# Long retention score products in all four quarters of the TensorE array

## Chip, cores, metric

One core of a Trainium2 chip. The metric is device time in microseconds (us) of one execution, median of several. The profiler's span of an execution is about 2 us shorter than its time.

## The reference

The first half is a retention layer over 4 batches, 8 heads, 768 tokens and head size 64; the second is a feed-forward layer with a leaky ReLU on 3072 tokens.

```python
for t in range(S):                       # gamma: one decay per head
    state = gamma * state + einsum('bhd,bhe->bhde', k[:, :, t], v[:, :, t])
    y[:, :, t] = scale * einsum('bhd,bhde->bhe', q[:, :, t], state)
x = y.transpose(0, 2, 1, 3).reshape(B * S, H * D)
h = x @ w_in                             # 512 -> 2048
out = maximum(0.01 * h, h) @ w_out       # 2048 -> 512
```

## The kernel before

The tokens go in 6 chunks of 128. Per chunk and batch the retention is: **scores** (keys by queries in the chunk, masked so that no query sees a later key), **reads** (state by queries), **values** (masked scores by v, added onto the reads in PSUM) and **state** (k by v). A key half of 64 tokens meets queries of 128 or, for the later half, 64 tokens, so a head has one long (128 columns) and one short (64 columns) score product. Two heads (j = 0, 1) lie in the two halves of the partitions.

```python
def scores_to(x, ps):
    for a in range(HP):                                   # HP = 4 pairs of heads
        for j in range(2):                                # long: rows j, columns j
            nc.tensor.matmul(halves(ps[j])[ts(j, 64), :, a, :],
                             lhsT=x[ts(j, 64), 1, a, 0:64], rhs=x[ts(j, 64), 0, a, :])
        for j in range(2):                                # short: rows j, columns 1 - j
            nc.tensor.matmul(halves(ps[j])[ts(1 - j, 64), 1, a, :],
                             lhsT=x[ts(j, 64), 1, a, 64:], rhs=x[ts(j, 64), 0, a, 64:])

def visit(c, b):                                          # a "plain visit", cut
    for f in (reads, first_values, last_values, state):
        for i in range(2):
            f(c, b + i)
    ...

def products_in_turn(b):                                  # the same four for chunk 1
    for f in (reads, first_values, last_values, state):
        for i in range(2):
            f(1, b + i)
```

Most batches of chunks 2 to 5 go through another form (a "visit with scores"): scores of a coming batch, reads of two batches, scores of another, then values and state. It is laid between the feed-forward products, which fill TensorE for the rest. In the profiles their groups are named A to D, with `_h` for the first feed-forward product and `_o` for the second. B_h, where it reads t, differences that DVE (VectorE) makes from the attention's output x, has to wait for DVE.

## Time and profile before

| | before |
|---|---|
| time, us | 664.34 |
| span of the profiled execution, us | 662.3 |
| TensorE busy | 99% |
| DVE busy | 57% |
| ScalarE busy | 27% |

A group line has the line of code, engine, operation, tiles and count, then busy time, mean ns of one, idle time ahead of it and what ended that. A line of the chain has start, length and what ran; the chain is followed back from the last instruction, so its pieces add up to the span. The prediction shows most lines of the profile before. Three more will be compared below, all from the chain in order of time: the products of the second pair of batches in chunk 1, and a later group B_h.

```profile
43.19 1.03 PE yp L224 x32
44.23 0.46 PE yp L241 x32
44.69 1.08 PE yp L249 x32
45.77 0.93 PE yp L264 x32
...
351.12 1.99 PE B_h L570 x8
```

L224 are the reads, L241 the first values, L249 the last values, L264 the state: 3.52 us from the first read to the next group, for two batches and without a pause. An undisturbed B_h group takes 1.73.

### The profile page before, as it was taken

To read this page: it belongs to the slowest core of one execution; us is meant where nothing else is said; L and a number is where in the kernel's file an instruction comes from. 1 tells how busy PE (TensorE), PEld (TensorE's weight loads), DVE (VectorE), ACT (ScalarE), POOL (GpSimd) and SP (SyncE) were. 2 spreads that over 40 slices of the span, in tenths; PEclk is the share of its full clock that TensorE was granted. 3 is DMA by queue.
4 is the path that set the end of the run, shared out by engine and by line. 5 is a ranking of instruction groups with operands and counts; after the bars stand their busy time and mean duration, and the time that the engine had idled before them with its cause. 6 is when DMAs were issued, how large, how long until landed. Compare 5 with 4: busy or idle time off the path is not lost.

```text
span 662.3 us, 11362 instructions
## 1 busy us (share of the span) xinstructions
PE 655.2 (99%) x4921; PEld 571.7 (86%) x4921; DVE 377.1 (57%) x635; ACT 176.3 (27%) x323; POOL 21.0 (3%) x25
## 2 busy tenths in 40 slices
PE   8999999999999999999999999999999999999998
PEld 5788888888888888888888888888888888888886
DVE  5789969889889594344437414537434344431342
ACT  4854555255261002202102211300220210221210
POOL 1000000000000020001001001000000100000000
PEclk9999999999999999999999999999999999999999
DMA  9921312322422650030023003005000101000001
GB/s 337 394 100 33 126 65 65 123 68 80 143 65 70 246 194 1 1 96 34 1 72 120 1 1 129 0 13 180 0 1 22 44 1 49 17 0 1 1 0 64
DMA packets 15761, 48.99 MB, mean 74 GB/s; under 512 B 1752, under 2 KB 2008, under 8 KB 15712
## 3 DMA queue, kind: packets, MB, share of 16 engines
q1 hardware_dynamic: 15408, 47.45, 20.6%
q8 instruction: 39, 0.64, 0.4%
q10 hardware_dynamic: 304, 0.81, 0.3%
q14 instruction: 10, 0.08, 0.0%
HBM read 41.97 MB, written 6.29 MB: 73 GB/s over the span
## 4 chain that ended last, share of the span: by engine, by line
PE 96%; ACT 1%; DVE 1%; DMA 1%; issue 0%; DVEq 0%
PE B_o L570 13%; PE A_o L570 13%; PE C_o L570 13%; PE A_h L570 12%; PE B_h L570 12%; PE C_h L570 12%; PE D_o L570 6%; PE D_h L570 6%; PE ap L176 2%; PE yp L249 2%; PE d L592 1%; PE yp L224 1%; PE sp L264 1%; DMA t<-decay_dram 1%; PE yp L241 1%; PE yp L264 0%
## 5 line engine op out<-in xcount | busy, mean ns | idle before, releaser
L570 PE MATMUL A_h<-x,w 128*128 128x256 f32 x368 | 87.7, 381 | 0.0
L570 PEld LDWEIGHTS A_h<-x,w 128*128 128x128 f32 x368 | 69.3, 190 | 9.7 <-issue 0.2
L570 PE MATMUL A_o<-g,w 128*128 128x256 f32 x288 | 68.1, 379 | 0.0
L516 DVE TENSOR_TENSOR m<-m,B_h 128x512 f32<-128x512 f32 x23 | 15.8, 686 | 88.4 <-PE B_h L570 88.4
L570 PEld LDWEIGHTS A_o<-g,w 128*128 128x128 f32 x288 | 54.6, 190 | 7.5
L610 ACT COPY m<-A_h 128x512 f32<-128x512 f32 x23 | 13.5, 586 | 174.5 <-PE A_h L570 154.3
L605 ACT ACTIVATE g<-g 128x512 f32<-128x512 f32 x69 | 42.0, 630 | 66.0 <-DVE g L516 66.0
L516 DVE TENSOR_TENSOR m<-m,B_o 128x512 f32<-128x512 f32 x16 | 11.0, 685 | 64.0 <-PE B_o L570 63.9
L570 PE MATMUL B_h<-t,w 128*128 128x256 f32 x184 | 44.3, 381 | 0.0
L570 PE MATMUL D_h<-t,w 128*128 128x256 f32 x184 | 43.5, 379 | 0.0
L570 PE MATMUL C_h<-x,w 128*128 128x256 f32 x184 | 43.5, 379 | 0.0
L570 PE MATMUL C_h<-t,w 128*128 128x256 f32 x184 | 43.5, 379 | 0.0
L570 PE MATMUL B_h<-x,w 128*128 128x256 f32 x184 | 43.5, 379 | 0.0
L570 PEld LDWEIGHTS B_h<-t,w 128*128 128x128 f32 x184 | 34.6, 190 | 6.0 <-DVE t L519 1.2
L570 PEld LDWEIGHTS D_h<-t,w 128*128 128x128 f32 x184 | 35.0, 190 | 4.8
L570 PEld LDWEIGHTS C_h<-x,w 128*128 128x128 f32 x184 | 35.0, 190 | 4.8
L570 PEld LDWEIGHTS C_h<-t,w 128*128 128x128 f32 x184 | 35.0, 190 | 4.8
L570 PEld LDWEIGHTS B_h<-x,w 128*128 128x128 f32 x184 | 35.0, 190 | 4.8
L150 POOL TENSOR_TENSOR kv<-kv,dec 128x512 f32<-128x512 f32 x18 | 19.9, 1105 | 496.4 <-DMA kv<-in_kv_dram 246.7
L519 DVE TENSOR_TENSOR gd<-g,gd 128x512 f32<-128x512 f32 x48 | 33.2, 692 | 1.7
L570 PE MATMUL B_o<-g,w 128*128 128x256 f32 x144 | 34.0, 379 | 0.0
L570 PE MATMUL C_o<-gd,w 128*128 128x256 f32 x144 | 34.0, 379 | 0.0
(137 smaller groups left out, 1060.8 us busy)
## 6 DMA issues: line engine op xcount, KB each, us to landing
raw<-in_weights_dram SPq DMA_DIRECT2D x31, 512.0 KB, 3.8
kv<-in_kv_dram SPq DMA_DIRECT2D x17, 512.0 KB, 5.0
out_dram<-o SPq DMA_DIRECT2D x23, 256.0 KB, 2.1
qk<-in_qk_dram SPq DMA_DIRECT2D x10, 512.0 KB, 4.6
o<-in_qk_dram SPq DMA_DIRECT2D x8, 512.0 KB, 4.6
in<-in_qk_dram SPq DMA_DIRECT2D x5, 512.0 KB, 8.5
in<-in_kv_dram SPq DMA_DIRECT2D x3, 512.0 KB, 8.1
in<-in_kv_dram SPq DMA_DIRECT2D x4, 256.0 KB, 8.1
```

The costliest lines, as they stand in the source:

```text
L150: engine.tensor_tensor(out=v, in0=v, in1=gk.unsqueeze(2).to_broadcast([128, H, D]), op=ALU.mult)
L176: nc.tensor.matmul(halves(ps[j])[ts(j, 64), :, a, :], lhsT=x[ts(j, 64), 1, a, 0:64], rhs=x[ts(j, 64), 0, a, :])
L224: nc.tensor.matmul(ps[ts(i, 64), j, m, :], lhsT=st[b][ts(j, 64), a, :], rhs=x[ts(j, 64), 0, a, :], start=(m == 0), stop=False, skip_group_ ...
L241: nc.tensor.matmul(ps[ts(i, 64), j, m, 0:64], lhsT=y[ts(j, 64), 1, 2 * a + j, :], rhs=am[ts(j, 64), 0, a, :], start=(c == 0 and m == 0), s ...
L249: nc.tensor.matmul(ps[ts(i, 64), j, m, 64:], lhsT=y[:, 1, 2 * a + j, :], rhs=am[:, 1 + j, a, :], start=False, stop=True, skip_group_check= ...
L264: nc.tensor.matmul(sp[ts(j, 64), a, :], lhsT=y[:, 0, 2 * a + j, :], rhs=y[:, 1, 2 * a + j, :], start=start, stop=True, skip_group_check=True)
L516: nc.vector.tensor_tensor(out=out, in0=a, in1=b, op=ALU.add)
L519: nc.vector.tensor_tensor(out=out, in0=a, in1=b, op=ALU.subtract)
L570: nc.tensor.matmul(half, lhsT=block(w, sa)[:, k, ts(i, 128)], rhs=rhs[:, k, :], start=(first and (i == 0 or split) and n == 0 and k == 0), ...
L592: nc.tensor.matmul(banks[r][:, i, :], lhsT=block(2 * u, r + 2 * kh)[:, k, ts(i, 128)], rhs=x[:, 2 * kh + th, k, :], start=(step == 0 and i ...
L605: nc.scalar.activation(g[:, i], g[:, i], AF.Prelu, alpha=0.01)
L610: nc.scalar.copy(out=got["m1"], in_=ps)
```

## The change

The intent: the long products of heads alternate between the diagonal quarters of the array (rows and columns of the same half) and the crossing ones (`s = i ^ j`, 0 or 1 by the head), so that each quarter of the array gets two long and two short products per batch instead of four of one kind. Two heads of opposite `s` then fit in three columns of 64 instead of four, so that one mask instruction covers what took three. The price: the first values now read from the other row half than the reads, into the same PSUM bank. So they go after the last values, a small ScalarE copy is put behind the reads to make TensorE finish them, and chunk 1 does one batch at a time.

```diff
     def scores_to(x, ps):
-        for a in range(HP):
-            ... (as above)
+        for m in range(HP // 2):
+            for i in range(2):
+                for late in range(2):
+                    for j in range(2):
+                        s, a = i ^ j, 2 * m + i
+                        to = (ps[j][ts(1 - s, 64), m, 1 + s] if late else
+                              ps[j][ts(s, 64), m, 0 : 2 + s : 1 + s])
+                        nc.tensor.matmul(to, lhsT=x[ts(j, 64), 1, a, ts(late, 64)],
+                                         rhs=x[ts(j, 64), 0, a, late * 64 :])
     def masked(c, b):                    # and masked_apart likewise
-        nc.vector.tensor_tensor(out=am[:, 1:3], ...)      # 128x512
-        for j in range(2):
-            masked_first(am, ps[:, j], j)                 # 64x256
+        nc.vector.tensor_tensor(out=am..., in0=scores[c, b]..., in1=mask..., op=ALU.mult)  # 128x768
     def reads(c, b):
         ...
+        nc.scalar.copy(out=between, in_=ps[:, :, 0 : HP // 2, 0:1])
     def first_values(c, b):
-                    lhsT=y[ts(j, 64), 1, 2 * a + j, :], rhs=am[ts(j, 64), 0, a, :]
+                    lhsT=y[ts(s, 64), 1, 2 * a + j, :], rhs=am[ts(s, 64), j, m, 0]
     def visit(c, b):
-        for f in (reads, first_values, last_values, state):
+        for f in (reads, last_values, first_values, state):
     def products_in_turn(b):
-        for f in (reads, first_values, last_values, state):
-            for i in range(2):
-                f(1, b + i)
+        reads(1, b)
+        values(1, b)                      # last values, then first values
+        reads(1, b + 1)
+        values(1, b + 1)
+        state(1, b)
+        state(1, b + 1)
```

## The prediction

> **What bounds the kernel now.** I read the page first (busy shares and the chain that ended last), then the groups by form, then the timeline around the score products, then the chain in order of time around each stage of the attention part.
>
> ```profile
> PE 655.2 (99%) x4921; PEld 571.7 (86%) x4921; DVE 377.1 (57%) x635; ACT 176.3 (27%) x323; POOL 21.0 (3%) x25
> PE 96%; ACT 1%; DVE 1%; DMA 1%; issue 0%; DVEq 0%
> ```
>
> TensorE (PE) is 99% busy and makes up 96% of the chain that set the end. So TensorE's own time counts one for one, and a saving elsewhere counts only where TensorE waits. TensorE waits in few places: the start (about 7 us), one wait of 1.8 us for a mask at 34 us, and three small ones at the weight load of B_h.
>
> The score products are these groups (176 of 384 instructions each; the rest read other tiles in the same shape):
>
> ```profile
> L176 PE MATMUL ap<-qk 64*64 64x128 f32 x176 | 11.6, 272 | 0.6 <-DMA qk<-in_qk_dram 0.6
> L179 PE MATMUL ap<-qk 64*64 64x64 f32 x176 | 9.6, 237 | 0.0
> ```
>
> The busy times of 11.6 and 9.6 us must not be added up as cost: the two kinds run at the same time. The timeline shows how they overlap:
>
> ```profile
> 230.97 0.28 PE L176 MATMUL ap<-o 64*64 64x128 f32 x2
> 230.98 0.27 PE L179 MATMUL ap<-o 64*64 64x64 f32 x2
> 231.08 0.28 PE L176 MATMUL ap<-o 64*64 64x128 f32 x2
> 231.09 0.23 PE L179 MATMUL ap<-o 64*64 64x64 f32 x2
> 231.19 0.28 PE L176 MATMUL ap<-o 64*64 64x128 f32 x2
> ```
>
> Two long products (128 columns) start together every 0.109 us, and the short ones (64 columns) start beside them. Before, the long ones all lie in two of the array's four 64x64 quarters, the short ones in the other two. A batch has 4 long products per quarter, each recorded as two instructions, so a long quarter is occupied 8 x 0.109 = 0.87 us per batch; the short quarters are idle about half of that. The chain agrees: both batches at 230.55 to 232.45 took 1.90 us, which is 16 x 0.109 = 1.74 plus 0.16 at the entry.
>
> The chain of one plain visit (two batches) prices the other products:
>
> ```profile
> 213.03 1.03 PE yp L224 x32
> 214.06 0.46 PE yp L241 x32
> 214.53 1.08 PE yp L249 x32
> 215.61 0.93 PE yp L264 x32
> ```
>
> The reads (L224, 128 columns) take 0.87 us where they follow other products of the same tile shape (at 237 us), and 1.03 here after full-array products: 0.16 for the change of shape. The first-half values (L241) follow in the same shape: 0.46, that is 14.4 ns per instruction, or 57.5 ns per short instruction in each quarter. L249 (128x64) after 64x64 is 1.08, L264 after L249 only 0.93: again 0.15 for the change. A full-array group of 8 costs 1.92 instead of 1.73 after small ones, 0.19. I use 0.16 per change.
>
> **What the Trainium skill says.** "TensorEngine Tiling (Array Packing)", Key Properties: tiles operate independently, and a change of tiling mode drains TensorE. The trace agrees: four quarters at once (the reads: 32 instructions in 0.87 us, 27 ns each, a quarter of 0.109), and 0.15 to 0.19 us per change of shape. "PSUM — Partial Sum Buffer", PSUM bank collisions: two writes from different row tiles into one bank and quadrant at once are an error. That explains the added ScalarE copy: the first-half values now come from the other row half than the reads into the same bank, so something must make TensorE finish the reads first. No run here shows the error itself. The same page, Engine vs sequencer instructions: ScalarE's queue is strict FIFO, so the copy stands behind whatever ScalarE has queued; in the trace ScalarE's long runs of work from 9.7 to 24.9 and 26.9 to 38.4 us are in program order.
>
> **The change, part by part.**
>
> Scores. The new order gives each quarter 2 long and 2 short products per batch: 4 x 0.109 + 4 x 0.056 = 0.66 us instead of 0.87, if a quarter can go on without the others. The order of issue is two long, two short on the crossing quarters, two long there, two short; with as little as one instruction queued per quarter behind the running one this packs without holes. Saving 0.21 us per batch. There are 24 batches: 16 of chunks 2 to 5 sit where TensorE is continuously busy, 4 of chunk 1 too; of chunk 0 only one counts (the others stand before waits for the decay table or for ScalarE's chain, which ends in w at 19.2 us). 21 x 0.21 = 4.5 us gross.
>
> Masks. Three DVE instructions per batch become one:
>
> ```profile
> L201 DVE TENSOR_TENSOR am<-ap,mask x12: 681/691/692, 7.0 to 233.1; 128x512 f32<-128x512 f32 x12
> L342 DVE TENSOR_TENSOR am<-ap,mask x24: 403/422/427, 237.2 to 511.6; 128x256 f32<-128x256 f32 x24
> L212 DVE TENSOR_TENSOR am<-ap,mask x48: 403/416/428, 7.6 to 512.0; 64x256 f32<-64x256 f32 x48
> ```
>
> 512 columns take 0.69 and 1024 take 1.22 us (the states at 25.1), so 768 take an estimated 0.96, against some 1.46 for the three back to back. DVE is not the bound, so this counts only at DVE waits: B_h waits for t in the three visits that also make differences (B_h 1.99 instead of 1.73, 0.26 each), and there one late mask stands ahead of t: 0.67 becomes about 0.48 (384 columns). Saving 3 x 0.19 = 0.6.
>
> The order of values in plain visits. Reads, last, first, state changes shape twice more than reads, first, last, state: 2 x 0.16 in each of the two plain visits of chunks 2 and 5. Cost 0.6. The visits with scores keep their order, and the next score product (0.66) stands between reads and values, so the copy is hidden there.
>
> The copy. In the trace a ScalarE copy of nearly this size is
>
> ```profile
> 7.63 0.17 ACT L807 COPY dec<-tables 128x12 f32<-128x12 f32 x1 [3.88 <-PE tables L804]
> ```
>
> 0.17 us, starting 0.04 after the products. From the last read's start: 0.27 to its end, 0.04, 0.17, some 0.05 back, and a weight load of 0.13 before the next product: about 0.6 after the reads stop issuing, in place of the 0.16 of a change of shape. In plain visits the second batch's reads cover it nearly (0.1 per visit, 0.2 in all). In chunk 1, now one batch at a time, nothing stands between: about 0.45 exposed per batch.
>
> Chunk 1. Per pair of batches without any stall: before 1.03 + 0.46 + 1.08 + 0.93 = 3.50. After: reads 0.60, last 0.62, first 0.39, the same three again at 0.44, 0.62, 0.39, state 1.08: 4.1, plus 2 x 0.45 exposed copy: 5.0. So the second pair loses 1.5. The first pair had this wait:
>
> ```profile
> 34.30 0.67 PE L224 MATMUL yp<-in,states 64*64 64x128 f32 x16 [1.77 <-DVE am L212]
> ```
>
> It goes, because the second mask ends some 1.5 us earlier and the first batch's values no longer stand behind it. But ScalarE is busy with weight conversion until about 32.3, and the first copy queues behind it: some 0.35 more. First pair: 5.5 before (31.95 to 37.45), about 5.35 after; gain 0.15.
>
> Chunk 0. Score and spread 0.21 earlier, which moves ScalarE's chain from 9.7 us on; one change of shape less before 24.5: 0.16. This 0.37 contains the one batch counted above.
>
> Sum. Start to 50 us: -0.37 (chunk 0), -0.85 (four scores of chunk 1), -0.15 and +1.5 (products): +0.1. After: -0.85 (four scores in output steps), -2.5 (twelve in visits with scores), -0.6 (B_h waits), +0.8 (plain visits): -3.1. Total -3.0: 664.35 becomes **661.3 us**, 0.5% less.
>
> **Rivals.**
>
> 1. The quarters are not independent: TensorE issues in order, and mixed long and short products wait for each other as pairs. For it: the skill's page on TensorE ("TensorE: Matmul & The Clock Gate", Part 3) calls matmuls strict FIFO in start and end. Against it: the trace has reads starting in idle quarters (236.74) before two earlier long score products (236.84), and short products hidden fully beside long ones. With no gain in the scores the total would be +1.4: 665.8. With half, 663.5.
>
> 2. The copy costs more than I give it in chunk 1, because ScalarE's queue then waits for TensorE (about 1.5 us idle between the two copies) and pushes decays and weight conversion back into TensorE's path. For it: ScalarE is busy 6.32 of the 6.45 us from 31.0 to 37.45. Against it: ScalarE is idle 4.8 us before 43.2. Some 1 to 2 us worse: 662.3 to 663.3.
>
> 3. DVE's saving of 0.5 us per batch is worth more in the first 50 us than I count: the converted weights and masks come earlier, and the chunk 1 stalls are smaller because some of the copy hides under shape changes that drain anyway. Then 660.
>
> **Range and chances.** The score term is firm to 0.5 if quarters are independent (I give that 85%). The chunk 1 term is the loose one, plus or minus 1. So 8 in 10: **659.7 to 663.0**. All of the attention products cost some 10% of the span, so a change of 2% (13 us) either way is almost out of reach: faster by over 2% 0.01, within 2% 0.98, slower 0.01.
>
> **What would show it.** Right: in the visits the long and short score products interleave so that 32 instructions take about 0.66 us in the chain (two batches at an output step about 1.5 instead of 1.90); B_h near 1.8; plain visits about 3.9 instead of 3.5; the 1.77 us mask wait gone; and in chunk 1 four waits of TensorE for ScalarE at last values, of 0.4 to 1 us. Wrong: score stages still 0.87 per batch (rival 1); TensorE waiting for decays or weights after 36 us (rival 2); the stages from 30 to 47 us shorter than before by more than 2 us (rival 3), or new waits in the visits with scores.

## The result, and the profile after

The changed kernel took 661.01 us (median of 6 runs, 660.91 to 661.24), the kernel before 664.34 in the same rounds: ratio 0.9952, 95% interval 0.9939 to 0.9965. The forecast was 661.3.

The page of the changed kernel, busy shares:

```profile
PE 652.0 (99%) x4921; PEld 568.4 (86%) x4921; DVE 360.5 (55%) x587; ACT 179.4 (27%) x343; POOL 20.4 (3%) x25
```

TensorE has as many instructions as before and 3.2 us less busy time, and it still is 96% of the chain: its work got denser. The chain in order of time shows where. First a score stage of two batches, then the plain visit of chunk 2 (L219 are the reads now), then the later B_h group:

```profile
230.48 1.49 PE ap L182 x48
...
212.65 1.03 PE yp L219 x32
213.69 1.08 PE yp L249 x32
214.77 0.62 PE yp L241 x32
215.39 1.08 PE yp L264 x32
...
349.29 1.81 PE B_h L571 x8
```

Scores went from 1.90 to 1.49 us, B_h from 1.99 to 1.81, and the plain visit from 3.50 up to 3.82: L241 and L264 each pay 0.15 to 0.16 more, because the tile shape changes ahead of each. The second pair of chunk 1:

```profile
41.78 0.64 PE yp L219 x16
42.42 0.02 issue
42.44 0.17 ACT between L224
42.62 0.04 issue
42.66 0.69 PE yp L249 x16
43.34 0.39 PE yp L241 x16
43.74 0.49 PE yp L219 x15
...
44.51 0.69 PE yp L249 x16
45.20 0.39 PE yp L241 x16
45.59 1.08 PE yp L264 x32
```

Here the ScalarE copy stands in the chain between the reads and the last values, and the pair takes 4.89 us instead of 3.52. (ACT is ScalarE.) One line of the timeline shows the longest such wait, where the copy queued behind ScalarE's weight conversion:

```profile
32.42 0.69 PE L249 MATMUL yp<-am,in 128*64 128x64 f32 x16 [0.70 <-ACT between L224]
```

The sum by place, from the chains of the two profiled executions: up to 48.6 us the gain is 0.03 us (48.63 against 48.60); there the scores' and the mask's gain in chunks 0 and 1 (1.0 us up to 37.4, 0.4 more by 39.8) is given back by the second pair. After that: four scores in two output steps -0.8, six visits with scores -0.39 each (the one at 236 from 5.24 to 4.85, the whole of it in its two scores), three B_h groups -0.19 each, and the two plain visits +0.31 in chunk 2 and +0.16 in chunk 5 (549.29 to 551.87 us before, 545.90 to 548.64 after). Chunk 5 has no state products, so there the new order adds one change of tile shape and not two. Together these make -3.3, against the measured -3.2.

### The profile page after: what moved, and what is told of

It is laid out like the page before. It is cut to its first block, busy times and chain, and to the rows that moved or that the text cites. A ratio compares the mean times of both kernels' runs of the same rounds, so it can differ in the third digit from the quotient of the medians.

```text
span 659.0 us, 11325 instructions
## 1 busy us (share of the span) xinstructions
PE 652.0 (99%) x4921; PEld 568.4 (86%) x4921; DVE 360.5 (55%) x587; ACT 179.4 (27%) x343; POOL 20.4 (3%) x25
## 4 chain that ended last, share of the span: by engine, by line
PE 96%; ACT 2%; DMA 1%; issue 0%; DVE 0%; ACTq 0%
PE B_o L571 13%; PE A_o L571 13%; PE C_o L571 13%; PE A_h L571 12%; PE B_h L571 12%; PE C_h L571 12%; PE D_o L571 6%; PE D_h L571 6%; PE ap L182 2%; PE yp L249 2%; PE yp L219 1%; PE d L593 1%; PE yp L241 1%; PE sp L264 1%; DMA qk<-in_qk_dram 1%; ACT in L154 1%
## 5 line engine op out<-in xcount | busy, mean ns | idle before, releaser
L571 PE MATMUL B_o<-gd,w 128*128 128x256 f32 x144 | 34.1, 379 | 0.0
```

Of the source, the lines that this page charges most:

```text
L571: nc.tensor.matmul(half, lhsT=block(w, sa)[:, k, ts(i, 128)], rhs=rhs[:, k, :], start=(first and (i == 0 or split) and n == 0 and k == 0), ...
```

## The experiments

Each kernel ran in 5 rounds beside the kernel before on its chip. The changed kernel itself ran again in the first set as a control:

> The changed kernel itself, unedited, so that the other runs of this chip have it beside them. Every theory expects 0.995 of the kernel before (661.0 us).

Measured 660.95 us, ratio 0.9952. As expected.

**Is it the even share, or the order of issue?**

```diff
-        for m in range(HP // 2):
-            for i in range(2):
-                for late in range(2):
-                    for j in range(2):
+        for cross in range(2):
+            for m in range(HP // 2):
+                for i in range(2):
+                    for j in range(2):
+                        late = i ^ cross
```

> The same score products, to the same places, in another order: all products of the two diagonal quarters of a batch first, then all of the two crossing quarters. Work per quarter is unchanged (2 long, 2 short). Theory A: the even share of work is enough, as each quarter takes its products from a deep queue: score stages stay at 0.65 us per batch, time 661.0. Theory B: TensorE issues in order and only one to three instructions queue behind a quarter's running one, so the gain comes from the alternation in the order of issue as much as from the even share: by that model 0.84 to 1.1 us per batch, so some 21 x 0.2 to 0.45 = 4 to 9 us slower than the changed kernel, 665 to 670.

Measured 666.76 us (ratio 1.0044), 5.8 us slower than the control and slower than the kernel before. Theory B holds. The chain, at the same score stage:

```profile
231.99 2.01 PE ap L183 x53
```

2.01 us instead of 1.49, with the same work in every quarter. A finer grouping was tried as well:

```diff
         for m in range(HP // 2):
-            for i in range(2):
-                for late in range(2):
+            for cross in range(2):
+                for i in range(2):
                     for j in range(2):
+                        late = i ^ cross
```

> As the run named order, but the diagonal quarters go first only within four heads at a time: blocks of eight instructions per side instead of sixteen. By the model of a queue of about three instructions per quarter (which fits the run named order, 2.01 us for two batches) such blocks cost 0 to 0.06 us per batch: 0 to 1.2 us slower than the changed kernel. Rival: any grouping costs in proportion, half of what order cost, 2.9 us slower.

Measured 661.39 us (0.9958), 0.4 us over the control of an earlier set, with the score stage at 1.55. The loss is not in proportion to the grouping, so the rival falls. A model in which TensorE issues in order and a quarter holds n instructions (one running; 0.109 us long, 0.056 short) gives for two batches 1.92 us at n = 3 and 1.65 at n = 4 in the coarse order, 1.43 and 1.32 in the fine one, and 1.32 in the order of the change; the measured stages hold 0.17 us of entry each, so they are 1.84, 1.38 and 1.32. A queue of three to four instructions per quarter fits all three to within 0.2 us. That is an estimate from three times, not a count, and no run separates the products from the weight loads that belong to them (0.13 us each for a short product in the trace before). What the two runs show is the effect of the order.

**What do the masks give?** The masks of the changed kernel were cut in three instructions again:

```diff
-        nc.vector.tensor_tensor(out=am..., in1=mask over 3 columns)            # whole
+        nc.vector.tensor_tensor(out=am[..., 1:3, :], in1=mask[:, 1:3]...)
+        for h in range(2):
+            nc.vector.tensor_tensor(out=am[half h, ..., 0, :], in1=mask[half h, 0]...)
```

> The changed kernel with its masks cut into three instructions again (in both forms), so only DVE's saving is undone. Theory: DVE counts only where TensorE waits for t: the B_h groups of three visits go from 1.80 back to 2.0 or a little over, the start loses up to 0.2 us: 0.7 to 1.0 us slower than the changed kernel, about 661.9. Rival 1: DVE is not the bound and its saving is worth nothing: 661.0. Rival 2: a large part of the gain came from DVE: 2 us or more slower.

Measured 663.01 us (0.9984), 2.06 slower than the control: more than I expected, and rival 2 seemed to hold. The profile shows two parts. The three B_h groups take 2.28 us instead of 1.80, from their start to the next group. And a pause is new, in the plain visit of chunk 2 (timeline):

```profile
219.25 1.99 PE L582 MATMUL B_o<-g,last 128*128 128x256 f32 x8 [0.86 <-DVE states L313]
```

The profile infers DVE's state instruction as releaser, but B_o reads nothing of the state, and in the changed kernel (run control) B_o started at 218.23 while the same DVE instruction ran to 218.99. What the pause fits better is told with the run costside below. So the cut was made only where B_h depends on it:

> As masksplit, but only the masks of the visits with scores are cut in three; those of one whole batch stay one instruction. In masksplit about half of the loss was a wait of B_o at 219 us for a state instruction that none of B_o's operands needs, the rest the three B_h groups (2.23 instead of 1.80). Theory: the B_h part is real and repeats: 3 x 0.43 = 1.3 us slower than the changed kernel, and B_o does not wait. Rival: B_o's wait follows from DVE being later overall and shows here too, 2 us slower.

Measured 662.30 us (five runs: three at 662.07 to 662.30, two at 663.56 and 663.81), ratio 0.9982. The three lower runs, the profiled one among them, are 1.1 to 1.4 us over the control's median, and B_o does not wait in the profile. (The profiled spans differ by only 0.8: this execution was 0.5 us ahead of the control's at 48 us, where the two kernels have the same code. Executions scatter by that much at the start.) The chain at the first of the B_h groups:

```profile
241.97 0.67 PE B_h L576 x2
242.65 0.03 issue
242.68 1.56 PE B_h L576 x6
```

The late mask now holds DVE for 0.95 us ahead of the last part of t (242.54 to 243.49) instead of 0.47 (242.52 to 242.99), and the group is 0.47 us longer. So DVE's time ahead of t is on the path, one for one: my cut made six mask instructions per batch where the kernel before had four, so 0.47 per group here against the 0.19 that the change itself moved. The two runs at 663.56 and 663.81 have no kept trace; the span of the second is 1.5 us longer, that of the first (660.5) hardly, so its surplus lies outside the span.

**What does the change pay?** The kernel before, with the copy, the new order of values and one batch at a time, but its own scores and masks:

```diff
+        nc.scalar.copy(out=between, in_=ps[:, :, 0 : HP // 2, 0:1])            # in reads
-        for f in (reads, first_values, last_values, state):                    # visit
+        for f in (reads, last_values, first_values, state):
-        (chunk 1: the four for both batches)
+        (chunk 1: reads, last, first of b; of b + 1; then both states)
```

> The kernel before (its scores and masks untouched) with only what the change pays: the ScalarE copy after the reads, the last values ahead of the first ones in plain visits and chunk 1, and chunk 1 one batch at a time. Theory: second pair of chunk 1 4.9 us instead of 3.5 (+1.4), first pair about even (-0.15, as the mask wait hides the copies), the two plain visits +0.3 each: 1.8 us slower than the kernel before, about 666. Scores and masks together are then worth some 5.1 us of which 1.8 is paid back. Rival: these parts cost nothing or help (the mask wait of 1.8 us in chunk 1 shrinks): within 0.5 us of before.

Measured 666.92 us (665.92 to 667.75; ratio 1.0038), 2.9 us slower than before by the median, 1.9 by the lowest run. The profiled run (667.75) again has a pause of TensorE behind the plain visit, this time inside A_o and with no releaser at all (chain):

```profile
220.05 1.33 issue
```

Without the pause the cost is close to the expected 1.8: by the chain +1.43 up to the end of chunk 1, and +0.31 and +0.16 in the plain visits of chunks 2 and 5, 1.9 in all. The rival (no cost) falls. I did not expect the pause. In both stalled executions the instruction queue's two transfers near this visit come later than in their unstalled counterparts (masksplit at 217 and 220 us, the control at 211 and 217; costside at 218 and 222, the kernel before at 214 and 218); that makes a late instruction fetch a candidate. The packed traces support it, read packet by packet. The pauses stand before neighbouring products of the program, the 1745th of TensorE in costside and the 1746th in masksplit, and TensorE goes on 1.37 and 1.25 us after the first of these transfers has landed (220.02 and 218.00 us). In the ten other readable traces it landed 2.7 to 6.2 us ahead of the 1745th product, and none pauses there. So the wait that the profile puts down to DVE in masksplit is probably none. No experiment shows the fetch to be the cause, nor why a transfer comes late.

**How much does the copy cost?** To leave it out where the last values stand between was built first and was refused: the check finds two row halves writing one PSUM bank with nothing to order them. So that can't be measured here. Instead it was made twice:

```diff
-        nc.scalar.copy(out=between, ...)
+        for _ in range(2):
+            nc.scalar.copy(out=between, ...)
```

> The changed kernel with the ScalarE copy after the reads made twice. Theory: the copy is exposed only where nothing stands between reads and values, in the four batches of chunk 1; there each second copy adds 0.2 us (0.17 and its start), and nearly nothing in plain visits and nothing in the twelve reads of visits with scores: 0.8 us slower than the changed kernel. Rival 1: it is exposed everywhere: 20 x 0.2 = 4 us slower. Rival 2: it hides under the change of tile shape that follows: 0.

Measured 662.14 us (0.9972), 1.2 slower than the control, not 0.8. Chunk 1 behaves as expected (each pair 0.39 longer, the second 5.28 instead of 4.89). What I missed are the plain visits: the one of chunk 2 is 0.19 us longer in the chain,

```profile
213.97 0.09 issue
214.06 1.18 PE yp L250 x32
```

so a single copy just fits under the second batch's reads, and anything longer shows. The visits with scores did not change (reads, values and state take 3.38 us there in the control's chain at 236 us, and 3.38 with two copies).

**One batch at a time.** Chunk 1 was put back to pairs, in the new order:

```diff
-        reads(1, b); values(1, b); reads(1, b + 1); values(1, b + 1); state(1, b); state(1, b + 1)
+        for f in (reads, last_values, first_values, state):
+            for i in range(2):
+                f(1, b + i)
```

> Only the third part of the change is undone: in chunk 1 the two batches of a pair go together again (reads, reads, last, last, first, first, state, state), so that one batch's reads stand in front of the other's wait for the ScalarE copy. Theory: one batch at a time is a loss, because nothing covers the copy and the tile shape changes oftener. Second pair 3.9 us instead of 4.89, first pair 0.6 us shorter (its second reads wait for the mask until 32.6, less than the copies cost), so 1.5 us faster than the changed kernel: 659.5. Rival: one batch at a time was made for a reason; together, the reads of the second batch wait for the second mask and everything behind them too, and the two orders come out within 0.3 us, or together is slower.

Measured 659.71 us (0.9934), 1.25 faster than the control. The second pair, in the chain:

```profile
41.46 1.03 PE yp L219 x32
42.50 1.08 PE yp L249 x32
43.58 0.62 PE yp L241 x32
44.20 1.08 PE yp L264 x32
```

3.82 us instead of 4.89, and no copy in it. The first pair gained 0.3 instead of 0.6, as I had left out 0.15 for the change of shape and the mask wait stayed at 0.9 us. So this part of the change was a loss; the rest of the change alone would have given it more.

**Fewer changes of shape.** On top of pairs, the state goes ahead of the first values:

```diff
-        for f in (reads, last_values, first_values, state):
+        for f in (reads, last_values, state, first_values):
```

> As pairs, and in chunk 1 and the plain visits the state products (128x64, like the last values) go ahead of the first values (64x64): one change of tile shape fewer in each of the two pairs of chunk 1 and in the plain visit of chunk 2 (chunk 5 has no state products). Theory: a change of shape costs TensorE 0.15 to 0.16 us whatever the data, so 3 x 0.155 = 0.45 us faster than pairs (1.25 faster than the changed kernel when measured): 1.7 faster than the changed kernel, about 659.2. Rival: the 0.15 us belong to the products' own start and stay: as pairs.

Four runs at 659.03 to 659.40, ratio 0.9929; a fifth, the profiled one, was disturbed (756 us at a clock of 0.851) and is left out. So it was run again:

> pairs_state unedited, since its profile fell in a stretch of lowered clock (0.851) and shows no usable stages. By its four undisturbed times it should be 659.4 again; theory: in the profile the second pair of chunk 1 takes 3.67 us (pairs: 3.82) and the plain visit of chunk 2 3.66 (changed kernel: 3.82). Rival: 3.82 in both, and the time as pairs.

Measured 659.31 us (0.9927). The plain visit of chunk 2 in the chain:

```profile
211.06 1.03 PE yp L219 x32
212.10 1.08 PE yp L249 x32
213.18 0.93 PE yp L264 x32
214.12 0.62 PE yp L241 x32
```

L264 is 0.93 again instead of 1.08: 3.66 for the visit, and 3.67 for the second pair of chunk 1, both as expected. The 0.15 us belong to the change of shape and go with it. The time moved by 0.4 us between two sets (659.71 to 659.31), as expected.

**A last step.** The second mask of chunk 1 ahead of the end of a weight conversion:

```diff
-    next_mantissas()
-    masked(1, 1)
+    begin_mantissas()
+    masked(1, 1)
+    end_mantissas()
```

> pairs_state, and in chunk 1 the second mask goes on DVE ahead of the last of the three steps of a weight conversion instead of behind it. In pairs TensorE waited 0.9 us for that mask (32.66). The scores that the mask needs are done at about 31.3, so the mask can end about 0.35 us earlier, at 32.2. Theory: 0.35 us faster than pairs_state, about 659.05. Rival: the conversion's end was on the path itself, through the queue of loads behind it: no gain or a loss.

Measured 659.29 us (0.9927), the same as pairs_state2. The mask did start and end earlier, and the chain was 0.26 us ahead at 300 us:

```profile
31.24 0.97 DVE am L204
...
32.25 0.67 PE yp L219 x16
```

but the profiled execution lost it at 345 us, in a pause that the profile puts down to nothing ("issue"). By the packets, an instruction transfer landed at 343.57 us here and at 343.50 in pairs_state2, and both kernels go on from there at 345.06: the lead may have gone into waiting for it. The times of the two kernels overlap, so no gain is shown. The best shown version is pairs_state2: 1.6 us faster than the change, 4.7 faster than before.

## Why the prediction was right

- **Scores.** 0.87 to 0.66 us per batch was forecast; 1.90 to 1.49 for two was measured (0.21 each), and 0.39 per visit with scores against 0.42. The reason given, quarters that go on without each other, holds with a limit (by the estimate above, a queue of three to four instructions); the prediction noted that one queued instruction is enough for this order, and the run with the coarse order shows what the order is worth: 5.8 us, more than the change.
- **Masks.** 0.6 us at B_h was forecast, 3 x 0.19 measured, and the masks cut again made the same groups longer. ("Three become one" holds for 12 of the 24 batches; in the visits with scores four became two.) The 768-column mask took 0.95 us (forecast 0.96).
- **Order of values.** +0.3 in each of two plain visits was forecast. In chunk 2 +0.31 was measured, and moving the state products took 0.15 away again. In chunk 5 it was +0.16: the prediction counted two more changes of shape where, without state products, there is one.
- **The copy.** Second pair of chunk 1: forecast 5.0, measured 4.89. TensorE waited for it four times, 0.70, 0.34, 0.28 and 0.34 us (forecast 0.4 to 1, so three a little under). The further 0.2 us that the prediction put on the two plain visits did not come: the copy fits there exactly, as the doubled copy shows.
- **First pair.** The 1.77 us mask wait went, and the copy behind ScalarE's queue took its place, as forecast: about 5.3 us for the pair (31.1 to 36.4) against 5.35.
- **Sums.** Up to 50 us +0.1 was forecast and -0.03 measured; after that -3.1 and -3.2. That both agree so closely is partly luck: executions scatter by 0.5 us up to there, and after it two misses offset each other (the plain visits cost 0.47 instead of 0.8, the visits with scores gave 2.3 instead of 2.5). Rival 2 (ScalarE's late work comes back into TensorE's path) did not happen: TensorE has no wait for it after 45 us. Rival 3 did not either.

What the prediction did not see is that chunk 1 one batch at a time was avoidable: it priced the loss (+1.5) and took it as part of the deal. Open is the cause of the pauses (0.86 and 1.33 us) in some executions of the edited kernels, though a late instruction transfer fits both.

## What to carry to other kernels

Where small products share the array, count the columns that each quarter streams and even them out, but alternate quarters in the order of issue every few instructions; here the order was worth more than the balance. A fix that needs an engine to be waited for costs nothing where other work of a batch already stands in between, and about 0.5 us per batch where nothing does (4.89 against 3.82 us for two, two more changes of tile shape included), so keep two batches interleaved around it. And group products by tile shape: each change cost 0.15 us, and moving one line removed it.

## What the Trainium skill lacked or had wrong

- "TensorE: Matmul & The Clock Gate", Part 3, has matmuls strictly first in, first out in start and end. Across quarters the starts in the kernel before do not keep to that: a read started at 236.74 while two score products earlier in the program started at 236.84. A queue of three to four instructions per quarter fits the stages of 1.49, 1.55 and 2.01 us; the page has no such depth per tile.
- "TensorEngine Tiling (Array Packing)", Key Properties, says that a change of mode drains TensorE and gives no cost: 0.15 to 0.19 us here. It doesn't say that the order of issue among tiles matters: 1.49 against 2.01 us for the same products.
- No page gives a length for pauses of TensorE such as the 1.33 us in the run costside. If a late instruction transfer is their cause, which no run shows, the point belongs to "Runtime: NRT & Kernel Launch", Instruction fetch mechanics.
